# Backward recurrence of a memory transformer: the V pass split 24 and 8 around dS's turning, fill pieces of 4 and 12 products, dout rows spread one step earlier

## The chip, the core and the metric

The kernel runs on one core of a Trainium2 chip. The metric is the device time of one execution in microseconds. A core has five engines that run beside each other: TensorE (PE; its weight loads are listed as PEld), VectorE (DVE), ScalarE (ACT), GpSimd (POOL) and SyncE (SP). Each has a queue of its own and works it off in order; semaphores join them. Matmuls write to PSUM, which has eight banks here: two are held for good by this kernel, six go round among all other sums.

## The reference

The kernel computes the output and all gradients of one pre-norm layer: a recurrent memory attention, then a gated feed-forward block. What the change touches is the gradient of the attention, which runs over the segments from the last to the first.

```python
def _A_ref(x, mem0, Wq, Wk, Wv, Wo, seg_len):        # x 1 x 2048 x 448, 16 heads of 256
    mem = mem0                                        # 8 memory rows
    for s in range(n_seg):                            # 64 segments of 32 rows
        h = concat([mem, x[s * 32:(s + 1) * 32]])     # 40 rows
        q, k, v = h @ Wq, h @ Wk, h @ Wv
        p = softmax(mask(q @ k.T * scale))
        o = (p @ v) @ Wo
        mem = o[:8]                                   # carried to the next segment
        outs.append(o[8:])
h  = x + _A_ref(layernorm(x), ...)
h2 = h + (silu(n @ w_gate) * (n @ w_up)) @ w_down     # n = layernorm(h)
# asked for: h2 and its gradients by x, mem0, Wq, Wk, Wv, Wo, w_gate, w_up, w_down
```

Because the memory rows go from segment to segment, the gradient of segment s needs the memory gradient that segment s+1 hands back: 64 steps in strict order.

## The kernel before, in words

The program has four stages one after the other: the forward recurrence, the feed-forward block with its gradients, the backward recurrence (`backward_chain`), and the weight gradients (`tail_phase`). The order of every engine's instructions is written out by hand: they are issued in the order in which the Python code emits them.

The backward recurrence runs one step per segment, from s = 63 to 0. Four segments make a tile t of 128 rows, and r = s mod 4. A step holds 32 rows that depend on the step before (8 memory rows and the first 24 of the segment); the last 8 rows of each of a tile's four segments (the B rows, 32 per tile) do not depend on the memory gradient of their own step, and their share of the work is done tile by tile, as filling between the pieces of a step. That filling is the dictionary `cur`, with named pieces `ua`, `ub`, `u2`, `u3` for TensorE and `e1`, `e3` for the evacuations; `late` and `late2` hold the transposes of the one and two steps ahead.

- `do_units(t)`: the product of the B rows of dout with Wo, 32 products of 512 columns in two sums; used in the step r = 2 (in segment 61 for the first tile). `u2` opens the second sum `p1`, `u3` closes it.
- `w_units(t, w)`: the B rows' share of the passes with Wv, Wk, Wq (r = 3, 1, 0), 32 products of 448 columns each, added up in the held sum `pob`.
- Segments 63, 62, 60 and 2 have no matmuls of this filling (63 has a piece of the stage before).

One step, in TensorE's order: `ua`; the projection of the gradient rows through Wo (L1364, 2 x 16 products of 512 columns, `proj`); `ub`; its transposes (L1370); the transposes that are late; dP (L1677, 32 products); `outer` for V (L1701, 32 small products into four banks); `u2`; half of the V pass (L1392, `w_pass`, 16 of 32 products of 448 columns; four of them lie side by side in the columns of the array); the turning of dS (L1727, 16 transposes); `outer` for K; the other half of the V pass; `outer` for Q; the K pass and the Q pass (32 products each); `u3`; the turning of the sum (L1399). All three passes add into one bank, `pH`.

The other engines around it: the softmax gradient is four operations of VectorE (L1681 to L1687) between dP and dS's turning. L1355 (VectorE, `V`) and L1358 (ScalarE, `A`) are the evacuations: those of `outer` for V are all ScalarE's, two large casts to dvA, two small ones to the B rows' buffer, and the same again; those for K and Q go to both in turn. `dST` is the evacuated turned dS, which `outer` for Q reads. The sum `pH` is copied in two parts (ScalarE, then VectorE), turned, and added up (L1404, `gsum`), and the memory rows of that go into `dA` for the next step's projection. In the next step VectorE copies the projection `dOev` into `dO_sb` (four copies of 32 x 512, then two), GpSimd does two more (L1652), and both halves of `doT` are filled, the first by VectorE.

GpSimd's queue at a step's start: L1752 copies the new memory rows to `dmem`; L1515 issues the load of P for the step after this one; L1621 copies the B rows of the tile into `doT`, which dP reads; in r = 3, `fill_tile` copies a tile's dout rows from the loaded `xl` to `dB` (L1541) and to the four places of the tile in `dA` (L1542), 24 rows each. `dA` has places for eight segments, so a tile's places are those of the tile two before it.

Of the kernel before, what the change touches and what calls it, by code (L numbers as in the profile page):

```python
# [265 lines left out]
def run_all(k: _K):  # L266
# [128 lines left out]
    with tc.manual_schedule():  # L395
# [83 lines left out]
        WT["o"] = W[3][:, 0:KC * HD].rearrange("p (c n) -> p c n", c=KC)  # L479
        tails = tail_phase(k, tail)  # L480
        back = backward_chain(k, WT, bwd, bwd, rstd1, dmem0T, tails)
        feed = ffn_phase(k, WT, ff, ffn, mv2, rstd2, {"o": Wo2, "v": Wv2, "k": Wk2, "q": Wq2}, back)
        k.feed = feed
# [848 lines left out]
def backward_chain(k: _K, WT, work, stage, rstd1, dmem0T, tails):  # L1332
    nc, tc = k.nc, k.tc
    S, D, M, H, Dh, HD = k.S, k.D, k.M, k.H, k.Dh, k.HD
    SEG, L, NSEG, NT, KC, DP, MC, DC = k.SEG, k.L, k.NSEG, k.NT, k.KC, k.DP, k.MC, k.DC
# [13 lines left out]
    def ps1(dtype=FP32):  # L1349
        if dtype == FP32:  # L1350
            return k.pspool.tile([P, 512], FP32, tag="ps", name="psf")
        return k.pspool.tile([P, 1024], BF16, tag="ps", name="psh")
# [4 lines left out]
    def A(out, in_):  # L1357
        nc.scalar.copy(out=out, in_=in_)  # L1358

    def proj(ps, stat, half, kcs=range(4)):  # L1360
        for kc in kcs:
            for g in range(G):
                c0 = g * GF + half * HB
                nc.tensor.matmul(ps[32 * g:32 * g + 32, :], lhsT=stat(kc), rhs=WoT_sb[:, kc, c0:c0 + HB],  # L1364
                                 start=(kc == 0), stop=(kc == KC - 1))

    def tr_half(ev, half):
        pt = ps1(BF16)
        for j in range(4):
            nc.tensor.transpose(pt[:, j * P:(j + 1) * P], ev[:, half * HB + j * P:half * HB + (j + 1) * P], ident[:, :])  # L1370
        return pt[:, 0:HB].rearrange("p (j g t) -> p j g t", j=4, g=G)

    def fm_view(dst, half, t0, t1):
        return dst[:].rearrange("p (g j) n -> p j g n", g=G)[:, 4 * half:4 * half + 4, :, t0:t1]
# [6 lines left out]
    WoT_sb, WvT_sb, WkT_sb, WqT_sb = WT["o"], WT["v"], WT["k"], WT["q"]  # L1381
    W = [k.Wall[:, i * KC * HD:(i + 1) * KC * HD] for i in range(4)]
    S_ps, pob = k.fix
# [4 lines left out]
    def w_pass(pO, WT, ch, i0, i1, first, last):  # L1388
        for i in range(i0, i1):
            c = ORDER[i]  # L1390
            g = i % 4
            nc.tensor.matmul(pO[32 * g:32 * g + 32, 0:D], lhsT=ch(c), rhs=WT[:, c, :],  # L1392
                             start=(first and i < 4), stop=(last and i >= MC - 4), skip_group_check=True)

    def turn(src, kcs=range(4)):
        y = ps1(FP32)
        for kc in kcs:
            c0 = min(kc * P, D - P)
            nc.tensor.transpose(y[:, kc * P:(kc + 1) * P], src[:, c0:c0 + P], identf[:, :])  # L1399
        return y[:, 0:DP].rearrange("p (c g n) -> p c n g", c=KC, g=G)  # L1400

    def gsum(out, in_):
        with nc.allow_low_precision("four float32 partial sums of one token"):
            nc.vector.tensor_reduce(out=out, in_=in_, axis=AX.X, op=ALU.add)  # L1404
# [11 lines left out]
    def none_units():  # L1416
        return {n: f_none for n in UNITS}

    def do_units(t):
        T = tiles[t]  # L1420
        st = {}

        def stat(kc):
            return T.dB[:, kc, :, :]

        def ua():
            st["p0"] = ps1(FP32)
            proj(st["p0"], stat, 0, range(0, 2))

        def ub():  # L1430
            proj(st["p0"], stat, 0, range(2, 4))

        def e1():
            T.dOB = stage.tile([P, GF], BF16, name="dOBev", tag="dOBev", bufs=2)
            A(T.dOB[:, 0:HB], st["p0"][:, :])

        def u2():
            st["p1"] = ps1(FP32)
            proj(st["p1"], stat, 1, range(0, 2))

        def u3():
            proj(st["p1"], stat, 1, range(2, 4))

        def e3():
            (A if t == NT - 1 else V)(T.dOB[:, HB:GF], st["p1"][:, :])

        def ut():
            T.doTB = stage.tile([P, MC, SEG], BF16, name="doTB", tag="doTB", bufs=2)
            A(fm_view(T.doTB, 0, 0, SEG), tr_half(T.dOB, 0))
            if t == NT - 2:  # L1450
                A(fm_view(T.doTB, 1, 0, SEG), tr_half(T.dOB, 1))

        def ut2():
            if t != NT - 2:
                A(fm_view(T.doTB, 1, 0, SEG), tr_half(T.dOB, 1))
        return dict(ua=ua, ub=ub, e1=e1, u2=u2, u3=u3, e3=e3, ut=ut, et=f_none, ut2=ut2, et2=f_none)

    def w_units(t, which):
        T = tiles[t]
        WT = {"v": WvT_sb, "k": WkT_sb, "q": WqT_sb}[which]  # L1460
        first, last = which == "v", which == "q"

        def ch(c):
            return T.dW[which][:, c, :]

        def ua():
            w_pass(pob, WT, ch, 0, 8, first, last)

        def ub():
            w_pass(pob, WT, ch, 8, 16, first, last)  # L1470

        def u2():
            w_pass(pob, WT, ch, 16, 24, first, last)

        def u3():
            w_pass(pob, WT, ch, 24, 32, first, last)

        def e3():
            A(partB[:, 0:D], pob[:, 0:D])

        if not last:
            return dict(none_units(), ua=ua, ub=ub, u2=u2, u3=u3)

        def half_turn(kcs):
            T.yB = turn(partB, kcs)

        def half_sum(kcs):
            for kc in kcs:
                gsum(T.dxnT[:, kc, :].rearrange("p (r j) -> p r j", r=4)[:, :, XA:SEG],
                     T.yB[:, kc, :, :].rearrange("p (r i) g -> p r i g", r=4))  # L1490
        return dict(ua=ua, ub=ub, e1=f_none, u2=u2, u3=u3, e3=e3, ut=lambda: half_turn((0, 1)), et=lambda: half_sum((0, 1)),
                    ut2=lambda: half_turn((2, 3)), et2=lambda: half_sum((2, 3)))

# [27 lines left out]
    def slot(s):  # L1521
        return s % NWIN

    def new_tile(t):
        o = Tok()
        o.t = t
        tiles[t] = o
        if t == NT - 1:
            o.xl = k.dlast[:].rearrange("p (c r n) -> p c r n", c=KC, r=4)
            return  # L1530
        o.xl = work.tile([P, KC, 4, SEG], BF16, name="dXl", bufs=1)
        if t == NT - 2:
            k.dnext = o.xl[:].rearrange("p c r n -> p (c r n)")
            return
        nc.gpsimd.dma_start(out=o.xl[:].rearrange("p c r n -> p (c r n)"), in_=dr["doutT"][t])

    def fill_tile(t):
        o = tiles[t]
        o.dB = stage.tile([P, KC, 4, M], BF16, name="dBx", tag="dBx", bufs=2)
        eng = nc.vector if t == NT - 1 else nc.gpsimd  # L1540
        eng.tensor_copy(out=o.dB[:], in_=o.xl[:, :, :, XA:SEG])  # L1541
        eng.tensor_copy(out=dA[:, :, slot(4 * t):slot(4 * t) + 4, M:SEG], in_=o.xl[:, :, :, 0:XA])  # L1542

    def open_tile(t):
        T = tiles[t]
        T.dxnT = stage.tile([P, KC, P], FP32, name="dxnT", tag="dxnT", bufs=3)
        T.dA = {w: stage.tile([P, MC, P], BF16, name="d" + w + "A", tag="d" + w + "A", bufs=1) for w in "vkq"}
        T.dmem = stage.tile([P, KC, 4, M], BF16, name="dmem", tag="dmem", bufs=2)
        o0 = MC * D + (t % 2) * MC * SEG
        T.dW = {w: W[i][:, o0:o0 + MC * SEG].rearrange("p (c n) -> p c n", c=MC) for i, w in enumerate("vkq")}  # L1550
# [46 lines left out]
    for s in range(NSEG - 1, -1, -1):  # L1597
        t, r = divmod(s, 4)
# [22 lines left out]
        nc.gpsimd.tensor_copy(out=doT[:, :, SEG:L], in_=T.doTB[:, :, r * M:(r + 1) * M])  # L1621
        if s == NSEG - 1:
            new_tile(t - 1)
        if r == (3 if t + 1 < NT else 2) and t > 0:
            fill_tile(t - 1)
        if r == 1 and t > 1:
            new_tile(t - 2)
# [3 lines left out]
        def stat(kc):  # L1631
            return dA[:, kc, slot(s), :]
# [14 lines left out]
        p1 = ps1()  # L1647
# [23 lines left out]
        for half in range(2):  # L1671
            for h in HEADS[half]:
                gg, hh = divmod(h, HG)
                for dc in range(DC):
                    c = h * DC + dc
# [40 lines left out]
        dvA, dkA, dqA = [T.dA[w][:, :, r * SEG:(r + 1) * SEG] for w in "vkq"]  # L1716
        outer(dO_sb, P_sb, dvA, T.dW["v"], (A, A, A, A), True)
        cur["u2"]()
        pH = ps1()
        w_pass(pH, WvT_sb, lambda c: dvA[:, c, :], 0, 16, True, False)  # L1720
        dST = work.tile([P, HG, L], BF16, name="dST", bufs=1)
        pts = []
        for gg in range(2):
# [5 lines left out]
        V(dST[0:L], pts[0][0:L, 0:HG * L].rearrange("p (h n) -> p h n", n=L))  # L1729
        A(dST[QB:NR], pts[1][QB:NR, 0:HG * L].rearrange("p (h n) -> p h n", n=L))  # L1730
        outer(Q_sb, dS, dkA, T.dW["k"], (V, A, V, A))
        w_pass(pH, WvT_sb, lambda c: dvA[:, c, :], 16, 32, True, False)
        if r == 0:
            nc.gpsimd.dma_start(out=dr["dVA"][t], in_=T.dA["v"][:].rearrange("p c n -> p (c n)"))
        outer(K_sb, dST, dqA, T.dW["q"], (V, A, V, A))
# [12 lines left out]
        if s >= 1:  # L1748
            gsum(dA[:, :, slot(s - 1), 0:M], y[:, :, 0:M, :])
            if r == 0:  # L1750
                open_tile(t - 1)
            nc.gpsimd.tensor_copy(out=tiles[(s - 1) // 4].dmem[:, :, (s - 1) % 4, :], in_=dA[:, :, slot(s - 1), 0:M])  # L1752
        else:
            gsum(dmem0T[:], y[:, :, 0:M, :])
        cur["e3"]()
# [326 lines left out]
```

## Time and profile before

| What | Value |
|---|---|
| Median of 3 runs | 2935.06 us (2926.3 to 2940.95) |
| The profiled execution | 2936.97 us, its span 2935.2 us |
| Mean granted TensorE clock | 0.980 |
| PE, DVE, ACT, POOL busy, of the span | 93%, 53%, 37%, 26% |
| Busy in 1313 to 2268 us (the backward recurrence): PE, DVE, ACT, POOL | 873, 574, 376, 246 us of 955 |
| DMA share in that stretch | 0.60 |

A row of the timeline reads: start, length, engine, line, operation, output<-input, shapes, how many instructions are merged into the row, and in square brackets how long the engine was idle before it and what ended that. Names: `arena` is one large SBUF buffer that holds nearly every tile, `wall` the buffer of the weights, `psf` and `psh` the banks that go round (float32, bfloat16), `s_ps` a held bank. A matmul's end is modelled, its start is measured. In the chain of waits, a row is start, length and the engine with its line, and "issue" is time for which nothing is shown.

### The profile page before, as it was taken

The page shows a single profiled execution, that of the slowest core. Times are in us where ns is not written, and L with a number is a line of the kernel's source. Part 1 is how long each engine was busy: PE and PEld are TensorE (multiplying, and loading weights), DVE is VectorE, ACT ScalarE, POOL GpSimd, SP SyncE. Part 2 cuts the span into 40 slices and gives each one's busy share as a digit, 9 for nine tenths or more (in the row PEclk, how much of TensorE's full clock was granted, in tenths as well). Part 3 has the DMA queues.
Part 4 walks back from the last instruction along what each step waited for, and adds up shares of the span by engine and source line. Part 5 has one row for each costly group of instructions (what it writes and reads, how often), then busy time and mean ns, then how long its engine had stood idle before and what let it go on. Part 6 is the DMA issues. An engine that isn't in the chain of part 4 may idle for free.

```text
span 2935.2 us, 104407 instructions
## 1 busy us (share of the span) xinstructions
PE 2722.7 (93%) x44384; PEld 1514.8 (52%) x44420; DVE 1561.3 (53%) x4196; ACT 1082.5 (37%) x2880; POOL 762.1 (26%) x1420
## 2 busy tenths in 40 slices
PE   3999999999998799987999999999999999999999
PEld 1555555555554455543555555555555454545454
DVE  4666666666665578874666666666665112222221
ACT  2444444444443455552444444434433111111110
POOL 2222222222222223321222222222222222233222
PEclk7999999999999899998999999999999999999999
DMA  9334434343435899997655655565556999999992
GB/s 273 116 123 134 126 123 137 116 130 122 135 116 140 217 218 233 245 226 166 151 156 153 189 152 161 155 175 152 161 151 215 334 228 227 209 225 241 204 224 69
DMA packets 652001, 515.86 MB, mean 176 GB/s; under 512 B 508592, under 2 KB 558112, under 8 KB 642000
## 3 DMA queue, kind: packets, MB, share of 16 engines
q1 hardware_dynamic: 600640, 309.09, 47.5%
q0 software_dynamic: 50896, 200.09, 20.5%
q8 instruction: 350, 5.73, 0.8%
q14 instruction: 115, 0.94, 0.1%
HBM read 145.89 MB, written 230.33 MB: 128 GB/s over the span
## 4 chain that ended last, share of the span: by engine, by line
PE 69%; DVE 15%; DMA 7%; issue 5%; SPq 2%; ACT 2%; POOL 1%; DVEq 0%; ACTq 0%; POOLq 0%
PE psf L1919 13%; PE psf L558 9%; PE psf L1392 9%; DVE arena L1355 5%; PE psf L687 4%; PE psf L1880 4%; PE psf L1105 3%; PE psf L1701 3%; PE psf L566 3%; PE psf L1364 2%; PE psh L572 2%; PE psf L1932 2%; PE psf L910 2%; PE psf L1399 2%; DMA wall<-in_A_Wv_dram 2%
## 5 line engine op out<-in xcount | busy, mean ns | idle before, releaser
L1919 PE MATMUL psf<-wall,arena 128*128 128x512 bf16 (+1 forms) x1788 | 390.6, 373 | 1.9
L521 ACT CAST arena<-psf 128x512 bf16<-128x512 f32 (+2 forms) x560 | 235.8, 453 | 362.4 <-PE psf L558 251.3
L1392 PE MATMUL psf<-wall,arena 128*32 128x448 bf16 x6144 | 336.8, 361 | 17.0 <-DMA wall<-in_A_Wq_dram 11.9
L1358 ACT CAST arena<-psf 128x256 bf16<-128x256 f32 (+1 forms) x597 | 233.0, 417 | 304.2 <-PE psf L1364 214.0
L558 PE MATMUL psf<-wall,arena 112*32 112x512 bf16 x5120 | 308.9, 384 | 31.0 <-DMA wall<-in_A_Wk_dram 14.0
L1919 PEld LDWEIGHTS <-arena 128*128 128x128 bf16 x1824 | 176.2, 98 | 198.3 <-issue 4.7
L1807 DVE CAST arena<-psf 128x448 bf16<-128x448 f32 (+1 forms) x83 | 54.7, 659 | 418.7 <-PE psf L1919 267.1
L518 DVE CAST arena<-psf 128x512 bf16<-128x512 f32 (+2 forms) x432 | 191.8, 469 | 123.7 <-PE psf L558 83.8
L1392 PEld LDWEIGHTS <-arena 128*32 128x32 bf16 x6144 | 154.9, 98 | 135.7 <-issue 30.7
L558 PEld LDWEIGHTS <-arena 112*32 112x32 bf16 x5120 | 126.4, 97 | 161.8 <-issue 28.2
L1355 DVE CAST arena<-psf 128x256 bf16<-128x256 f32 (+1 forms) x339 | 164.8, 486 | 83.0 <-PE psf L1701 41.8
L1805 ACT CAST arena<-psf 128x512 bf16<-128x512 f32 (+1 forms) x75 | 42.2, 563 | 427.9 <-PE psf L1919 267.0
L566 PE MATMUL psf<-wall,arena 112*32 112x512 bf16 x2560 | 169.2, 385 | 9.4 <-DMA wall<-in_A_Wv_dram 9.4
L1364 PE MATMUL psf<-wall,arena 128*32 128x512 bf16 x2560 | 156.6, 381 | 1.2 <-DVE arena L1404 1.2
L521 ACT COPY arena<-psh 40x160 bf16<-40x160 bf16 (+2 forms) x320 | 119.2, 400 | 94.6 <-PE psh L670 52.8
L1752 POOL COPY arena<-arena 128x32 bf16<-128x32 bf16 x63 | 13.2, 210 | 541.5 <-DVE arena L1404 541.5
L1701 PE MATMUL psf<-arena 40*128 40x40 bf16 x6144 | 146.9, 178 | 3.2 <-issue 1.8
L687 PE MATMUL psf<-wall,arena 128*32 128x224 bf16 x5120 | 147.6, 265 | 1.1 <-issue 1.1
L524 POOL COPY arena<-arena 32x512 bf16<-32x512 bf16 x129 | 77.8, 603 | 267.9 <-ACT arena L521 264.2
L1701 PEld LDWEIGHTS <-arena 40*128 40x128 bf16 x6144 | 125.8, 93 | 33.8 <-issue 16.2
L1355 DVE COPY arena<-arena 32x512 bf16<-32x512 bf16 x384 | 133.8, 349 | 8.8
L1355 DVE COPY arena<-psf 128x192 f32<-128x192 f32 x64 | 22.9, 358 | 215.2 <-ACT arena L1358 215.2
(223 smaller groups left out, 4475.5 us busy)
## 6 DMA issues: line engine op xcount, KB each, us to landing
Vtok<-arena SPq DMA_DIRECT2D x128, 192.0 KB
KtokA<-arena SPq DMA_DIRECT2D x64, 256.0 KB
QtokA<-arena SPq DMA_DIRECT2D x64, 256.0 KB
OTA<-arena POOLq DMA_DIRECT2D x16, 1024.0 KB, 5.2
arena<-QtokA SPq DMA_DIRECT2D x128, 128.0 KB
arena<-KtokA SPq DMA_DIRECT2D x128, 128.0 KB
dVA<-arena POOLq DMA_DIRECT2D x16, 1024.0 KB, 5.2
dKA<-arena POOLq DMA_DIRECT2D x16, 1024.0 KB, 7.2
```

What stands on the lines that cost most here:

```text
L518: nc.vector.tensor_copy(out=out, in_=in_)
L521: nc.scalar.copy(out=out, in_=in_)
L558: nc.tensor.matmul(ps[32 * g:32 * g + 32, :], lhsT=stat(kc), rhs=W_sb[0:DB, kc, c0:c0 + HB], start=(kc == 0), stop=(kc == KC - 1))
L566: nc.tensor.matmul(ps[32 * g:32 * g + 32, :].rearrange("t (y d) -> t y d", y=2), lhsT=stat(kc), rhs=wv[:, x, :, half, e, :], start=(kc == ...
L687: nc.tensor.matmul(ps[32 * g:32 * g + 32, 0:2 * DB], lhsT=x, rhs=Wo_sb[:, c, a * 2 * DB:(a + 1) * 2 * DB], start=first, stop=last)
L1355: nc.vector.tensor_copy(out=out, in_=in_)
L1358: nc.scalar.copy(out=out, in_=in_)
L1364: nc.tensor.matmul(ps[32 * g:32 * g + 32, :], lhsT=stat(kc), rhs=WoT_sb[:, kc, c0:c0 + HB], start=(kc == 0), stop=(kc == KC - 1))
L1392: nc.tensor.matmul(pO[32 * g:32 * g + 32, 0:D], lhsT=ch(c), rhs=WT[:, c, :], start=(first and i < 4), stop=(last and i >= MC - 4), skip_gr ...
L1701: nc.tensor.matmul(po[:, n * L:(n + 1) * L], lhsT=lhs[b:b + L, lc:lc + P], rhs=rhs[b:b + L, hh, 0:L], start=True, stop=True)
L1880: nc.tensor.matmul(ps[:, 0:D], lhsT=stat[:, i, c * P:(c + 1) * P], rhs=Y[:, i, 0:D], start=(i == 0), stop=(i == kts - 1))
L1919: nc.tensor.matmul(ps[:, 0:N], lhsT=Hx[:, i, dc * P:(dc + 1) * P], rhs=X[:, i, b * N:(b + 1) * N], start=(i == 0), stop=(i == kts - 1))
```

## The change

Four edits in the backward recurrence.

1. The V pass runs 24 products ahead of dS's turning and 8 behind `outer` for K; it was 16 and 16.
2. `u2` of `do_units` does one quarter of the second sum (4 products) and `u3` three (12); they did 8 and 8.
3. `u2` of `w_units` does 4 products and `u3` 12; they did 8 and 8.
4. The dout rows of a tile are spread (`fill_tile`) at the end of the step ahead, that is in r = 0, behind the copy to `dmem`; it was done in r = 3, behind the copy to `doT`. In segment 62 it stays where it was.

```diff
         def u2():
             st["p1"] = ps1(FP32)
-            proj(st["p1"], stat, 1, range(0, 2))
+            proj(st["p1"], stat, 1, range(0, 1))
         def u3():
-            proj(st["p1"], stat, 1, range(2, 4))
+            proj(st["p1"], stat, 1, range(1, 4))
...
         def u2():
-            w_pass(pob, WT, ch, 16, 24, first, last)
+            w_pass(pob, WT, ch, 16, 20, first, last)
         def u3():
-            w_pass(pob, WT, ch, 24, 32, first, last)
+            w_pass(pob, WT, ch, 20, 32, first, last)
...
-        if r == (3 if t + 1 < NT else 2) and t > 0:
+        if s == NSEG - 2:
             fill_tile(t - 1)
...
-        w_pass(pH, WvT_sb, lambda c: dvA[:, c, :], 0, 16, True, False)
+        w_pass(pH, WvT_sb, lambda c: dvA[:, c, :], 0, 24, True, False)
...
-        w_pass(pH, WvT_sb, lambda c: dvA[:, c, :], 16, 32, True, False)
+        w_pass(pH, WvT_sb, lambda c: dvA[:, c, :], 24, 32, True, False)
...
             nc.gpsimd.tensor_copy(out=tiles[(s - 1) // 4].dmem[:, :, (s - 1) % 4, :], in_=dA[:, :, slot(s - 1), 0:M])
+            if r == 0 and t > 1:
+                fill_tile(t - 2)
```

## The prediction

> **What bounds the kernel now.** I read the page's chain of waits first, then the same chain in order of time for a stretch of the backward recurrence, then the timeline around the lines that the change touches.
>
> ```profile
> PE 69%; DVE 15%; DMA 7%; issue 5%; SPq 2%; ACT 2%; POOL 1%; DVEq 0%; ACTq 0%; POOLq 0%
> ```
>
> The columns are engines and their shares of the chain. TensorE carries 69% of it, and yet 15% runs through VectorE: within one backward step the two alternate. The chain of a plain step (segment 49, r = 1; start, length, engine and line) shows where.
>
> ```profile
> 1541.52 0.50 DVE arena L1687
> 1542.02 0.04 issue
> 1542.06 0.49 PE psh L1727 x16
> 1542.56 0.67 PE psf L1701 x32
> 1543.22 0.87 PE psf L1392 x16
> 1544.09 0.67 PE psf L1701 x32
> 1544.76 3.17 PE psf L1392 x64
> ...
> 1548.00 0.38 ACT arena L1358
> ...
> 1548.43 0.83 PE psf L1399 x4
> ```
>
> From dS (L1687) on, everything up to the step's end is in series: dS is turned (L1727), outer(k), the second half of the V pass (16 products, 0.87), outer(q), the K and Q passes, the copy of the sum, its turning (L1399). So whatever TensorE does between dS's turning and the step's end that could have been done earlier is on the path; what it does while it waits for dS is free. Price of a product of the pass: 48 more of them cost 3.17 - 0.87 = 2.30, so 0.048 each, 0.19 for a group of four, and the 16 in 0.87 hold 0.10 of change-over to the next kind of matmul.
>
> **Part 1: the V pass, 24 before and 8 behind.** Eight products, 8 x 0.048 = 0.38, leave the path behind dS in every step. What must be shown is that they fit ahead of it.
>
> ```profile
> 1540.45 0.56 PE L1392 MATMUL s_ps<-wall 128*32 128x448 bf16 x8
> 1540.84 0.93 PE L1392 MATMUL psf<-wall,arena 128*32 128x448 bf16 x16
> 1542.06 0.49 PE L1727 MATMUL psh<-ident,arena 40*40 40x40 bf16 x16 [0.30 <-DVE arena L1687]
> ...
> 1540.19 0.65 ACT L1358 CAST arena<-psf 128x256 bf16<-128x256 f32 x2 [0.40 <-PE psf L1701]
> 1540.72 0.35 ACT L1358 CAST wall<-psf 128x64 bf16<-128x64 f32 x2
> 1540.93 0.69 ACT L1358 CAST arena<-psf 128x256 bf16<-128x256 f32 x2
> ```
>
> The wait before the turning shows as 0.30, behind the pipeline's tail. By starts, 16 products from 1540.84 are issued by 1541.61, and dS comes for 1542.06: 0.45 free. The fill piece u2 shrinks from 8 to 4 products, so the pass can begin at 1540.45 + 0.19 = 1540.64; 24 products are issued by 1540.64 + 1.15 = 1541.79, with the change-over 1541.89, still 0.17 before dS. Two new waits lie here. The pass starts 0.2 earlier and needs the first cast of dvA: two casts take 0.65 from 1540.19, the first should be done near 1540.56 (estimate, half way and a little); if both were needed, as at worst, it would begin at 1540.84 as now and be through at 1542.09, which costs 0.03. And products 17 to 24 need the third cast (first of the pair at 1540.93, about 1541.35); they come up at 1540.64 + 0.77 = 1541.41. Behind these waits on TensorE stands only the turning, which waits for dS anyway. Cost ahead of dS: nothing, cover 0.17.
>
> Behind dS, outer(q) comes up at 1543.64 instead of 1544.02 and must find banks and its operand.
>
> ```profile
> 1542.65 0.42 ACT L1358 COPY arena<-psh 40x320 bf16<-40x320 bf16 x1 [0.79 <-PE psh L1727]
> ...
> 1543.36 0.22 ACT L1358 CAST wall<-psf 128x64 bf16<-128x64 f32 x1
> ...
> 1543.23 0.21 DVE L1355 CAST wall<-psf 128x64 bf16<-128x64 f32 x1
> ...
> 1543.69 0.21 DVE L1355 CAST wall<-psf 128x64 bf16<-128x64 f32 x1
> ```
>
> dST is complete at 1543.07. If banks go round in the order in which they come free, outer(q)'s four take those freed at 1543.07, 1543.44, 1543.58 and 1543.90, and are wanted at 1543.64, 1543.81, 1543.98 and 1544.15 (0.67 for four): none late, the narrowest by 0.2. The evacuations of outer(q) and the passes behind it move along. So a plain step gains 0.38.
>
> **Part 2: the fill pieces at the end.** u3 has 12 products instead of 8, while the sum is copied.
>
> ```profile
> 1547.72 0.55 PE L1392 MATMUL s_ps<-wall 128*32 128x448 bf16 x8
> ...
> 1591.09 0.60 PE L1364 MATMUL psf<-wall,arena 128*32 128x512 bf16 x8
> 1591.80 0.44 PE L1399 MATMUL psf<-identf,arena 128*128 128x128 f32 x2
> ```
>
> Plain step: 12 x 0.048 from 1547.72 end at 1548.30, with the change-over at 1548.40, and the turning starts at 1548.43 because it waits for ScalarE. Free, by 0.03. In the dout step (r = 2, pieces of 512 columns, 0.055 each) 12 end at 1591.75, with the change-over 1591.85, against 1591.80: 0.05 to 0.08 late.
>
> The dout step is also the one where the front is full.
>
> ```profile
> 1583.59 0.61 PE L1364 MATMUL psf<-wall,arena 128*32 128x512 bf16 x8
> 1584.15 0.94 PE L1392 MATMUL psf<-wall,arena 128*32 128x448 bf16 x16
> ...
> 1583.87 0.35 ACT L1358 CAST wall<-psf 128x64 bf16<-128x64 f32 x2
> ...
> 1585.18 0.39 PEld L1727 LDWEIGHTS <-arena 40*40 40x40 bf16 x16 [0.54 <-DVE arena L1687]
> ```
>
> Its pass starts 0.56 after u2, where eight products of 0.055 fill 0.44. I read this as the wait of pH for a bank: u2's own sum p1, the half-turned dxn and outer(v)'s four hold all six until ScalarE's first small cast (about 1584.10). A shorter u2 then brings nothing: 24 products from 1584.15 end at 1585.30, with the change-over 1585.40, and the turning is 0.22 later than 1585.18. The dout step so gains 0.38 - 0.22 - 0.06 = 0.10.
>
> Sum of both parts: 45 plain steps with fill (r = 3, 1, 0 of tiles 14 to 0) and four without any (63, 62, 60, 2): 49 x 0.38 = 18.6. Dout steps: 14 x 0.10 = 1.4, and segment 61, where no half-turned dxn holds a bank, 0.3. Together 20.3 us.
>
> **Part 3: the spreading of dout one step earlier.**
>
> ```profile
> 1539.13 0.72 PE L1677 MATMUL s_ps<-arena 128*40 128x40 bf16 x32 [0.29 <-POOL arena L1652]
> 1553.32 0.75 PE L1677 MATMUL s_ps<-arena 128*40 128x40 bf16 x32 [0.25 <-POOL arena L1652]
> 1568.11 0.72 PE L1677 MATMUL s_ps<-arena 128*40 128x40 bf16 x32 [0.84 <-POOL arena L1652]
> 1582.25 0.76 PE L1677 MATMUL s_ps<-arena 128*40 128x40 bf16 x32 [0.25 <-POOL arena L1652]
> ...
> 1563.98 0.21 POOL L1752 COPY arena<-arena 128x32 bf16<-128x32 bf16 x1 [3.40 <-DVE arena L1404]
> 1564.51 0.56 POOL L1515 DMA_DIRECT2D arena<-P_all  x1 [0.32 <-issue]
> 1565.07 0.41 POOL L1621 COPY arena<-arena 128x256 bf16<-128x256 bf16 x1
> 1565.40 0.30 POOL L1541 COPY arena<-arena 128x128 bf16<-128x128 bf16 x1
> 1565.64 0.51 POOL L1542 COPY arena<-arena 128x384 bf16<-128x384 bf16 x1
> 1565.73 1.78 DVE L1355 COPY arena<-arena 32x512 bf16<-32x512 bf16 x4
> ...
> 1565.73 0.56 DVE L1355 COPY arena<-arena 32x512 bf16<-32x512 bf16 x1
> ...
> 1566.71 0.64 POOL L1652 COPY arena<-arena 32x512 bf16<-32x512 bf16 x1 [0.57 <-ACT arena L1358]
> ...
> 1580.47 1.18 DVE L1355 COPY arena<-arena 32x512 bf16<-32x512 bf16 x4
> ```
>
> From dP to dP a step takes 14.19 (1539.13 to 1553.32) but 14.79 into the r = 3 step, where dout is spread (L1541, L1542). The reason stands in the VectorE rows: its four copies of dO take 1.78 beside the spreading (1565.73) and 1.18 without it (1580.47), and dP waits for what follows them. (The releaser POOL L1652 is named because its copy ends near by; it writes nothing that dP reads.) The next step, 1568.11 to 1582.25, is 14.14, 0.05 short of 14.19, so 0.05 of the 0.60 comes back. The spreading now goes behind L1752 and ahead of the load of P and the copy to doT in POOL's queue. If they follow without a gap: L1541 and L1542 end at 1564.19 + 0.81 - 0.14 (each copy starts 0.07 before the last one ends) = 1564.86, P's load at 1565.42, doT's copy at 1565.82. It is read by dP at 1568.11; P's load is for a step later: neither is late. By the records doT's copy overlaps VectorE's first copy by 0.09. But the first copy now ends at 1565.73 + 0.56 = 1566.29, 0.30 (1.18 over four) after 1565.99, while L1542's record ends at 1566.15: VectorE is let in some 0.16 before the record's end, and for doT's copy that is 1565.66, in time. The fourth copy then starts near 1566.62, just ahead of POOL's own copies at 1566.71. So I take the whole: 0.60 - 0.05 = 0.55, 14 times, 7.7 us. Bounds: 0.60 if nothing comes back, and 0 if the 0.32 that POOL now idles before L1515 stays in line.
>
> The rows show the two engines shutting each other out rather than sharing. The Trainium skill (SBUF — State Buffer, "Who interferes with whom") says so: a VectorE copy in a two-port mode and a GpSimd instruction hold the port pair in turn, each for its whole length, and who issues first wins. Taken to the letter, doT's copy would hold off VectorE's first copy by 0.09 and part 3 would give 14 x 0.46 = 6.4 instead of 7.7. It also speaks against the move: its box on SWDGE lets a DMA of the POOL queue starve while VectorE copies, and P's load moves 0.9 towards those copies; no run here shows that.
>
> **Sum.** 20.3 + 7.7 = 28.0 us. The profiled execution took 2936.97 (span 2935.2), 0.07% over the median of 2935.06; so 2909 for a profiled one and about **2907** for the median.
>
> **Rivals.**
> A. The spreading gives nothing: its 0.81 plus the 0.32 idle push doT's copy to 1566.1, under VectorE's copies, and the fourth meets POOL L1652 as now. For it: the slack of only 0.1 or so. Against: L1515 starts 0.53 behind L1752's start, and two more copies in between would cover that. Time: 2907 + 7.7 = 2915. The Trainium skill's rule (same page) of who issues first speaks for it.
>
> B. Behind the turning the banks decide, not TensorE: outer(q) waits until all of outer(k) is evacuated. VectorE's last small cast ends at 1543.90 and ScalarE's should be near it, so outer(q) stays at about 1544.0, plain steps win nothing and dout steps lose 15 x 0.28 = 4. For: the bank wait that I read in dout steps. Against: the order of banks counted above. Time: 2935 + 4 - 7.7 = 2931.
>
> C. The other side: the bank wait of the dout step holds in plain steps too, and B holds behind it. Then the pass starts no earlier than ScalarE's first small cast, about 1541.0, 24 products run to 1542.25, the turning is 0.19 late and nothing behind it is won: 49 x 0.19 + 15 x (0.22 + 0.06) = 13.5 lost, 2941 with part 3 and 2949 without. It decides once the pass in plain steps starts later than 1540.81. Against: the pass now starts 0.39 after u2, exactly its eight products.
>
> D. The moved spreading blocks the next projection, which reads the same tile: POOL ends at 1564.86, the projection starts near 1563.9, 1.0 x 14 = 14 lost, 2907 + 7.7 + 14 = 2929. Against: today it is emitted ahead of the projection too, and that one starts long before L1541.
>
> **How the numbers follow.** Forecast as summed 0.60; A 0.22; B 0.06; C 0.07, more than half of it without part 3; D 0.05. A measurement of this kernel tells 0.5%, 14.7 us, from no change: below 2920.4 counts as faster, above 2949.7 as slower. Faster: the forecast, A, and the near ends of B and D, 0.85. Same: the rest of B and D, and C with part 3, 0.10. Slower: C without part 3, and what I do not see, 0.05. The range: runs of before lie 8.8 below and 5.9 above their median, so 2898 at the low end; up to 2922 it holds A and its scatter.
>
> **What would show it.** The wait of L1727 for L1687 falls in plain steps and is gone in dout steps, where L1687 ends before the turning by 0.2 more. Outer(q) follows outer(k) after about 0.49 instead of 0.87. The interval dP to dP is 13.8 in plain steps, also into r = 3, about 14.4 behind dout steps. VectorE's four copies take about 1.2 in every step. Wrong if outer(q) starts with idle time before it on banks, if L1399 waits for TensorE, or if four copies at 1.8 remain.

## Result and the profile after

| What | Before | After | Ratio, 95% interval |
|---|---|---|---|
| Median of 11 runs each, side by side | 2937.65 us | 2916.11 us | 0.994 [0.9918, 0.9962] |
| The changed kernel again (6 runs), beside before (29) | 2925.34 us | 2901.89 us | 0.9909 [0.988, 0.9937] |
| And a third time (6 runs, beside 17) | 2927.35 us | 2902.94 us | 0.991 [0.9889, 0.9932] |

The change is faster by 0.6 to 0.9%, 18 to 27 us by the ratios; the medians differ by 21.5, 23.5 and 24.4 us. The forecast, 28 us, is a ratio of 0.9904: inside the two later intervals, below the first.

The profiled execution of the changed kernel took 2919.64 us, its span 2917.9, which is 17.3 less than before. By the first and the last dP, the backward recurrence runs from 1320.8 to 2233.5 us, 912.6; before it ran from 1313.5 to 2253.75, 940.2. It is 27.6 shorter, but that this comes so near the forecast is in part luck: 5.4 of it lie in the step of segment 63 alone, which took 35.05 here before, 29.65 after, and 28.2 to 30.6 in all other profiles of both kinds. The stages ahead of the recurrence ended 7.3 later in this profile and the tail is 3.0 longer; the change touches neither, and over all profiles of this study the first dP lies between 1302.7 and 1323.5. So one pair of profiles says little by its spans. I read the step's parts first, then the steps, then the sum.

The shares of the chain, the whole kernel after:

```profile
PE 70%; DVE 13%; DMA 7%; issue 5%; SPq 2%; ACT 1%; POOL 1%; another core or an unknown queue 0%; DVEq 0%; ACTq 0%; POOLq 0%
```

VectorE's share fell from 15% to 13%: part of TensorE's work moved beside it. The chain in order of time, the same plain step (segment 49):

```profile
1537.29 0.50 DVE arena L1687
1537.79 0.04 issue
1537.84 0.49 PE psh L1727 x16
1538.33 0.67 PE psf L1701 x32
1538.99 0.49 PE psf L1392 x8
1539.49 0.67 PE psf L1701 x32
1540.15 3.14 PE psf L1392 x64
1543.30 0.57 PE s_ps L1392 x12
1543.86 0.80 PE psf L1399 x4
```

Outer(q) follows outer(k) after 0.49 instead of 0.87, and the turning still starts 0.05 after dS, so 24 products do fit ahead of it. ScalarE's copy has left the chain: u3 with 12 products now ends with it (0.57 from 1543.30), as the 0.03 of cover said. L1399 still starts 0.06 behind the end of that copy (1543.40 to 1543.77), as it did before, so u3 does not hold it back.

The starts of dP, timeline of TensorE:

```profile
1534.90 0.73 PE L1677 MATMUL s_ps<-arena 128*40 128x40 bf16 x32 [0.28 <-POOL arena L1652]
...
1548.71 0.75 PE L1677 MATMUL s_ps<-arena 128*40 128x40 bf16 x32 [0.25 <-POOL arena L1652]
...
1562.53 0.75 PE L1677 MATMUL s_ps<-arena 128*40 128x40 bf16 x32 [0.25 <-POOL arena L1652]
...
1576.34 0.76 PE L1677 MATMUL s_ps<-arena 128*40 128x40 bf16 x32 [0.25 <-POOL arena L1652]
```

The intervals are 13.81, 13.82 and 13.81; the second is the one into r = 3, and TensorE's wait of 0.84 ahead of that dP is now 0.25. Medians over the steps without a stall, by the r of the step in which the interval begins:

| Kernel | r = 3 | r = 2 (dout) | r = 1 | r = 0 (into r = 3) | a tile |
|---|---|---|---|---|---|
| before | 14.14 | 14.48 | 14.19 | 14.80 | 57.61 |
| after | 13.82 | 14.31 | 13.81 | 13.82 | 55.76 |

A tile gains 1.85 us; the prediction's steps make it 3 x 0.38 + 0.10 + 0.55 = 1.79.

The spreading, timeline of GpSimd and VectorE from the end of a step r = 0 into r = 3:

```profile
1559.00 0.21 POOL L1752 COPY arena<-arena 128x32 bf16<-128x32 bf16 x1 [3.40 <-DVE arena L1404]
1559.15 0.29 POOL L1541 COPY arena<-arena 128x128 bf16<-128x128 bf16 x1
1559.38 0.50 POOL L1542 COPY arena<-arena 128x384 bf16<-128x384 bf16 x1
1559.84 0.56 POOL L1515 DMA_DIRECT2D arena<-P_all  x1
...
1560.39 0.41 POOL L1621 COPY arena<-arena 128x256 bf16<-128x256 bf16 x1
1560.75 1.18 DVE L1355 COPY arena<-arena 32x512 bf16<-32x512 bf16 x4
1561.73 1.44 POOL L1652 COPY arena<-arena 32x512 bf16<-32x512 bf16 x2 [0.93 <-ACT arena L1358]
```

GpSimd runs them without a gap (the 0.32 of idle time before L1515 is covered), and VectorE's four copies take 1.18, no longer 1.78. DoT's copy ends at 1560.80 by its record, 0.05 after VectorE's first copy began, and holds nothing off.

The dout step, timeline of TensorE, VectorE and ScalarE:

```profile
1577.69 0.40 PE L1364 MATMUL psf<-wall,arena 128*32 128x512 bf16 x4
...
1577.96 0.35 ACT L1358 CAST wall<-psf 128x64 bf16<-128x64 f32 x2
...
1578.25 1.32 PE L1392 MATMUL psf<-wall,arena 128*32 128x448 bf16 x24 [0.16 <-ACT wall L1358]
...
1578.73 0.49 DVE L1687 SCALAR_TENSOR_TENSOR arena<-arena 104x320 bf16<-104x320 f32 x1
...
1579.50 0.49 PE L1727 MATMUL psh<-ident,arena 40*40 40x40 bf16 x16
...
1585.03 0.82 PE L1364 MATMUL psf<-wall,arena 128*32 128x512 bf16 x12
1585.31 0.37 ACT L1358 COPY arena<-psf 128x256 f32<-128x256 f32 x1 [2.58 <-PE psf L1392]
...
1585.78 0.79 PE L1399 MATMUL psf<-identf,arena 128*128 128x128 f32 x4
```

The profile now names the bank wait that the prediction read: the pass idles 0.16, and what ends it is ScalarE's small cast to `wall`. DS is there at 1579.22 and the turning starts at 1579.50, 0.28 behind it, where a plain step has 0.05: 0.23 late. At the step's end L1399 starts 0.10 after ScalarE's copy (1585.68), where plain steps have 0.06.

One thing the prediction has no term for. Windows from the dP of segment 62 to that of segment 0 (the window, its length, busy time of PE, PEld, DVE, ACT, POOL, granted clock, DMA share, GB/s), before and after:

```profile
1348.60:2253.80 905.20, 841.03 (x19691) 487.16 (x19691) 555.18 (x1560) 363.27 (x1299) 236.83 (x470) 0.99 0.57 158
```

```profile
1350.50:2233.50 883.00, 840.91 (x19691) 487.74 (x19691) 550.76 (x1559) 364.29 (x1300) 238.95 (x472) 0.99 0.60 162
```

TensorE is busy for the same 841 us, so the 22 us are idle time that was taken out. But some idle time has come in. Waits of 1313 to 2268 us, before and after (us, times, longest):

```profile
PEld L1727 <- DVE arena L1687: 43.1, 63, 0.9
...
PE psh L1727 <- DVE arena L1687: 13.6, 48, 0.5
...
PE psf L1392 <- issue: 4.5, 3, 2.2
```

```profile
PEld L1727 <- DVE arena L1687: 31.4, 63, 0.7
...
PE psf L1392 <- issue: 7.0, 6, 3.2
```

The wait for dS fell, as forecast (its second row is gone after). "Issue", time for which nothing is shown, grew: it comes in stalls between like matmuls. One of them, timeline of TensorE, segment 24:

```profile
1892.09 3.02 PE L1392 MATMUL psf<-wall,arena 128*32 128x448 bf16 x58
1897.14 0.55 PE L1392 MATMUL psf<-wall,arena 128*32 128x448 bf16 x6 [2.04 <-issue]
```

Call excess what the intervals from the dP of segment 59 to that of segment 0 hold above the median of their r (that of the steps without a stall, as in the table), where it is over 0.15: 10.7 us in this profile of before, 16.6 in this one of after.

### The profile page after: what moved, and what is told of

Its sections match the earlier page's. It is cut to its first block, busy times and chain, and to the rows that moved or that the text cites. A ratio compares the mean times of both kernels' runs of the same rounds, so it can differ in the third digit from the quotient of the medians.

```text
span 2917.9 us, 104401 instructions
## 1 busy us (share of the span) xinstructions
PE 2727.5 (93%) x44420; PEld 1515.5 (52%) x44420; DVE 1555.8 (53%) x4196; ACT 1082.6 (37%) x2880; POOL 763.4 (26%) x1420
## 4 chain that ended last, share of the span: by engine, by line
PE 70%; DVE 13%; DMA 7%; issue 5%; SPq 2%; ACT 1%; POOL 1%; another core or an unknown queue 0%; DVEq 0%; ACTq 0%; POOLq 0%
PE psf L1921 13%; PE psf L558 9%; PE psf L1392 8%; DVE arena L1355 5%; PE psf L687 4%; PE psf L1105 3%; PE psf L1882 3%; PE psf L1701 3%; PE psf L566 3%; PE psf L1364 3%; PE psh L572 2%; PE psf L1934 2%; PE psf L910 2%; PE s_ps L1392 2%; PE s_ps L1185 2%
## 5 line engine op out<-in xcount | busy, mean ns | idle before, releaser
L1392 PEld LDWEIGHTS <-arena 128*32 128x32 bf16 x6144 | 147.9, 98 | 134.2 <-issue 30.2
```

## The experiments

Theory: each of the four edits does what the prediction's steps say (T). The rivals are A, B, C and D of the prediction.

**One part alone.** E1 has only the split of the V pass (edit 1), e2 only the pieces (edits 2 and 3), e3 only the spreading (edit 4).

```diff
# e1
+        w_pass(pH, WvT_sb, lambda c: dvA[:, c, :], 0, 24, True, False)
...
+        w_pass(pH, WvT_sb, lambda c: dvA[:, c, :], 24, 32, True, False)
# e2
+            proj(st["p1"], stat, 1, range(0, 1))     # u3: range(1, 4)
...
+            w_pass(pob, WT, ch, 16, 20, first, last) # u3: 20, 32
# e3
+            if r == 0 and t > 1:
+                fill_tile(t - 2)
```

> Only edit 1: V pass 24 and 8, pieces 8 and 8, spreading in r = 3 as before. My theory (the pass behind dS's turning is on the path, banks do not decide): with u2 still 8 products the pass begins at the old place, 24 products end 0.03 after dS, so plain steps fall from 14.19 to 13.84 from dP to dP, the step into r = 3 from 14.80 to 14.45, the dout step from 14.48 to about 14.32; sum about 49 x 0.35 + 15 x 0.16 = 19.5 us. Rival (outer(q) waits for the evacuation of outer(k), banks decide): plain steps stay at 14.2 or rise, sum 0 or a loss.

> Only edits 2 and 3: pieces 4 and 12, V pass 16 and 16, spreading as before. My theory: the pass begins 0.19 earlier and waits that much longer for dS, and u3's third group fits into the copy of the sum: plain steps stay at 14.19, the wait of L1727 for L1687 grows by 0.19; the dout step is 0.02 to 0.08 longer; sum 0 to 1 us lost. Rival (TensorE's work at the end is not covered): plain steps 0.19 longer, 9 us lost.

> Only edit 4: dout rows spread at the end of r = 0. My theory: the step into r = 3 falls from 14.80 to 14.19, the one behind it rises by 0.05 to 14.19, VectorE's four copies take 1.2 instead of 1.8; sum 14 x 0.55 = 7.7 us. Rival A (the copy to doT takes the place of the spreading beside VectorE's copies): into r = 3 stays at 14.8, sum 0. Rival D (the projection waits for the spreading): into r = 3 about 15.2.

| Kernel | Ratio, 95% interval | r = 3 | r = 2 | r = 1 | r = 0 |
|---|---|---|---|---|---|
| e1, split | 0.9944 [0.9925, 0.9964] | 13.83 | 14.31 | 13.82 | 14.45 |
| e2, pieces | 1.0019 [0.9997, 1.0042] | 14.14 | 14.48 | 14.19 | 14.80 |
| e3, spreading | 0.9981 [0.9959, 1.0003] | 14.20 | 14.48 | 14.19 | 14.20 |

The split carries the gain of the steps. The pieces change no interval, not even the dout step's, for which 0.02 to 0.08 more had been expected; with the split they are worth about 0.01 in a step (13.83 to 13.82, 13.82 to 13.81). The spreading takes 0.60 out of the interval into r = 3 and gives 0.06 back in the next, as the prediction had it from one place of the old trace. By time alone e3 can't be told from nothing; its intervals can, in the timeline of e3's TensorE:

```profile
1533.96 0.75 PE L1677 MATMUL s_ps<-arena 128*40 128x40 bf16 x32 [0.25 <-POOL arena L1652]
...
1548.16 0.75 PE L1677 MATMUL s_ps<-arena 128*40 128x40 bf16 x32 [0.25 <-POOL arena L1652]
```

These are the dP of segments 48 and 47: 14.20 into r = 3, where before had 14.79 in the same place. A and D fall; C falls with e1, which has no step that is longer than before, and so does B for 24 products, since plain steps do win.

**The bank wait of the dout step.** E5 is the changed kernel with `u2` put behind the 24 products in the dout step, so that `pH` takes its bank ahead of `u2`'s sum.

```diff
+        late_u2 = r == 2 and t > 0 and t + 1 < NT
+        if not late_u2:
-        cur["u2"]()
+            cur["u2"]()
         pH = ps1()
         w_pass(pH, WvT_sb, lambda c: dvA[:, c, :], 0, 24, True, False)
+        if late_u2:
+            cur["u2"]()
```

> The changed kernel, but in the dout steps (r = 2, tiles 14 to 1) pH and its 24 products are emitted ahead of u2, so that pH takes the sixth bank and p1 the next free one. My theory (the pass waits there for a bank): it starts some 0.15 to 0.2 earlier, u2 fits behind it, the turning comes about 0.16 sooner and the dout step falls from 14.31 to 14.15; other steps stay; 2 us in all. Rival (the pass waits for dvA's casts or for the change-over, not for a bank): the pass starts where it did, u2 behind it delays the turning by 0.2 more, 14.5.

Measured: 2899.32 against 2925.73 us, 0.9908 [0.9881, 0.9935], and 14.16 behind dout steps. TensorE's timeline of such a step in e5 (L1731 is the turning):

```profile
1562.46 1.35 PE L1392 MATMUL psf<-wall,arena 128*32 128x448 bf16 x24
1563.64 0.39 PE L1364 MATMUL psf<-wall,arena 128*32 128x512 bf16 x4
1563.96 0.49 PE L1731 MATMUL psh<-ident,arena 40*40 40x40 bf16 x16
```

The pass starts without idle time, and the turning starts 3.00 behind dP (1560.96) instead of 3.16 (1579.50 less 1576.34). So it was the bank. This is the best version of the study by its steps, by 0.15 in each of 14 steps, 2 us; the time does not separate it from the change.

**More products ahead.** E6 runs 28 products ahead of the turning and 4 behind, e7 all 32 ahead. Behind the turning TensorE's own work would shrink by 0.19 and 0.38 more.

```diff
# e6
-        w_pass(pH, WvT_sb, lambda c: dvA[:, c, :], 0, 24, True, False)
+        w_pass(pH, WvT_sb, lambda c: dvA[:, c, :], 0, 28, True, False)
...
-        w_pass(pH, WvT_sb, lambda c: dvA[:, c, :], 24, 32, True, False)
+        w_pass(pH, WvT_sb, lambda c: dvA[:, c, :], 28, 32, True, False)
# e7: 0, 32 and no second w_pass
```

> The changed kernel with 28 products ahead and 4 behind. My theory: in plain steps 28 products end 0.02 to 0.1 after dS and 0.19 leaves the path behind it, banks are still free in time: 13.81 falls to 13.65 to 13.72. In dout steps 0.19 is lost ahead and won behind: 14.31 stays. Together 5 to 8 us faster than the change. Rival B (the banks of outer(k) decide behind the turning): plain steps no shorter, or longer.

> The changed kernel with all 32 products ahead of the turning and none behind. If TensorE alone decided behind the turning: turning 0.2 late, 0.49 won behind it (eight products and a change-over): plain steps 13.54. By my reading of the banks (outer(q)'s last two wait for the third and fourth evacuation of outer(k)): about 13.84, with idle time of TensorE inside outer(q). Dout steps 14.5 to 14.7.

Measured: e6 0.9949 [0.9927, 0.9971], plain steps 13.82 to 13.85, dout 14.39. E7 0.9975 [0.9955, 0.9994], plain steps 14.01 to 14.04, dout 14.58. The gain I expected of e6 did not come, and e7 is worse than I gave it by either reading. The timeline of TensorE and ScalarE in a plain step of e6:

```profile
1539.76 0.37 PE L1392 MATMUL psf<-wall,arena 128*32 128x448 bf16 x4
...
1540.06 0.92 PE L1701 MATMUL psf<-arena 40*128 40x40 bf16 x32
...
1540.34 0.24 ACT L1358 CAST wall<-psf 128x64 bf16<-128x64 f32 x1
...
1540.91 0.75 PE L1392 MATMUL psf<-wall,arena 128*32 128x448 bf16 x12
```

Outer(q) starts 4.34 behind dP (1535.72) in e6 and 4.52 in the changed kernel, 0.18 earlier, but takes until the K pass 0.85 instead of 0.66: all of it is lost again. Its last quarter starts at 1540.63, 0.05 after ScalarE's last small cast of outer(k) ends (1540.58). The same stretch of the changed kernel, TensorE and ScalarE (the last row from a window cut at that point):

```profile
1538.26 0.73 PE L1701 MATMUL psf<-arena 40*128 40x40 bf16 x32
...
1539.42 0.73 PE L1701 MATMUL psf<-arena 40*128 40x40 bf16 x32
1539.50 0.24 ACT L1358 CAST wall<-psf 128x64 bf16<-128x64 f32 x1
...
1540.08 0.75 PE L1392 MATMUL psf<-wall,arena 128*32 128x448 bf16 x12
...
1539.80 0.36 PE L1701 MATMUL psf<-arena 40*128 40x40 bf16 x11
```

There the cast ends at 1539.74 and the quarter starts at about the same 0.05 behind it. So 24 and 8 is just where the banks begin to bind; rival B's mechanism is real, and stands one group of four further on. In e7 nothing lies between the two outer products, and both stand in TensorE's timeline as one row:

```profile
1526.69 0.49 PE L1727 MATMUL psh<-ident,arena 40*40 40x40 bf16 x16
1527.11 1.89 PE L1701 MATMUL psf<-arena 40*128 40x40 bf16 x64
1528.93 2.26 PE L1392 MATMUL psf<-wall,arena 128*32 128x448 bf16 x44
```

1.82 from outer(k)'s start to the K pass, where the changed kernel needs 1.82 with eight products of the V pass between them (1538.26 to 1540.08): the eight products were free there. And the turning is 0.2 late as well (3.14 behind dP at 1523.55, where the changed kernel has 2.94).

**The stalls.** In the eleven profiles of kernels that store tile by tile (all but e8 and e11), every pause of over 0.8 us between the starts of two matmuls of one line lies, in segments 59 to 1, in a step of r = 0, which issues the three stores of a tile's dVA, dKA and dQA, 1 MB each, or in the step r = 3 behind it (43 pauses, 0.8 to 2.7 us). E8 is the changed kernel with these stores moved behind the recurrence, e11 the kernel before with the same. Both store the last tile's buffers in every other tile's place, so they leave out the other tiles' part of the gradients of Wq, Wk and Wv and serve for times alone. Their total times hold the stores at the end and are not compared with the others.

```diff
-        if r == 0:
+        if s == 0:
             nc.gpsimd.dma_start(out=dr["dVA"][t], ...)   # and dKA, dQA
...
+    for tt in range(1, NT):
+        for x in "vkq":
+            nc.gpsimd.dma_start(out=dr["d" + x.upper() + "A"][tt], ...)
```

> The changed kernel, but the stores of dVA, dKA and dQA of tiles 15 to 1 (3 MB each tile, in r = 0) are sent together behind the last step, all from the last tile's buffers; the whole is some 200 us longer for that, only the steps 59 to 0 are read. In six profiles all stalls of TensorE over 0.6 us (issue) lie in steps r = 0 and r = 3. Theory S: the tile's stores bring them: they are gone, excess over the regular steps falls from 12 to 15 us to under 4. Rival: they come from the supply of instructions alone and stay where they are (segments 32, 28, 24).

> The kernel before with the stores of dVA, dKA and dQA of tiles 15 to 1 sent behind the last step (from the last tile's buffers; longer as a whole for that), to be held against the same with the change, whose steps 59 to 0 took 825.1 us with 2.4 of excess. Both theories: regular steps as before (849 us), excess under 4, so 850 to 853 for steps 59 to 0: the whole difference of 25 to 28 us stands where no stalls are.

Measured: 3022.75 us for e8 and 3058.91 for e11 as a whole. From dP of segment 59 to dP of segment 0:

| Kernel | us | excess |
|---|---|---|
| before with its stores at the end (e11) | 849.7 | 1.4 |
| after with its stores at the end (e8) | 825.1 | 2.4 |
| before, mean of two profiles (859.6, 853.5) | 856.6 | 7.8 |
| after, mean of three profiles (838.5, 837.1, 836.6) | 837.4 | 15.5 |

The windows of e8 over that stretch:

```profile
1377.70:2202.80 825.10, 794.02 (x18781) 461.55 (x18782) 525.13 (x1487) 346.35 (x1237) 205.96 (x408) 1.00 0.45 111
```

Without the stores (DMA share 0.45, not 0.60) the change takes 24.6 us out of these 59 steps, and next to no excess is left in either. With them it takes 19.1. So the stalls come with the stores, and 5.5 us of the steps' gain go back into them. Segment 0, whose own stores stay in place in e8 and e11, keeps its pause in all thirteen profiles (1.3 to 3.5 us).

What TensorE lacks in a pause no row of the timeline names, but the trace's DMA packets do. One queue carries instructions (number of packets, MB, share of the 16 engines; the same in before and after):

```profile
q8 instruction: 350, 5.73, 0.8%
```

These 350 packets of 16 KB go with some 89 700 instructions of PE and PEld: 64 bytes each, 256 to a packet. Counted through, TensorE goes on after each of the 43 pauses at the same place of such a block of 256 (instruction 193 or 194), and 1.25 to 1.61 us behind the end of a packet of this queue. So what it waits for is its next instructions. The packets come late: one starts a median of 0.8 to 1.0 us after TensorE has begun the block ahead, but in the eleven profiles 162 start more than 2.5 and up to 5.2 us after that, every one of them in r = 0 or r = 3; in e8 and e11 none starts more than 2.2 after it. A block lasts about 5.7 us. So theory S and its rival are both half of it: the instructions run short, and they do so beside the stores.

**Repeats.** E4 and e10 are the changed kernel again, e9 is the kernel before.

> The changed kernel once more, for a second profile. From dP to dP the steps saved 28 us where nothing unusual happens, but the measured gain is some 20. Theory X: the rest is scatter of TensorE's rare stalls of 1 to 4 us (issue) and of the stages ahead and behind, which differ from execution to execution: the regular steps are again 13.81, 14.31, 13.81, 13.82, the stalls sum to something else than 15 us (before: 11), and the stages outside are within 10 us of both profiles. Theory Y: the denser steps cause more stalls: the sum is again 15 or more.

> The kernel before once more, for a second profile of it. So far the excess of steps 59 to 0 over the regular ones was 10.7, 7.4 and 8.7 us in the three profiles with 16 products ahead, and 15.1, 14.5, 12.0, 10.6, 10.2 and 13.7 in the six with 24 or more. Theory Y (denser steps give part of the gain back as stalls, 3 to 4 us): 7 to 11 here. Theory X (scatter): anywhere from 7 to 15. The ratio is 1.

> The changed kernel a third time, for its ratio: 0.994 [0.9918, 0.9962] and 0.9909 [0.988, 0.9937] so far. Steps alone (28 us) would give 0.9905; with 3 to 4 us of stalls given back (theory Y) 0.9918. The regular steps are 13.81, 14.31, 13.81, 13.82; excess by Y 10 to 15, by X anywhere from 7.

E4 and e10 stand in the first table; their intervals are 13.82, 14.31, 13.81 and 13.82 again. E9 gave 0.9997 [0.9974, 1.0019] against before, which is how well this comparison tells no change. Excess in all profiles with the stores in place: 16 products ahead 10.7, 7.5, 9.7 and 4.8 (before, e2, e3, e9), mean 8.2; 24 or more ahead 16.6, 14.6, 15.1, 12.1, 13.3, 13.7 and 14.6 (after, e1, e4 to e7, e10), mean 14.3. (The expectations give lower figures for some, as 15.1 for after: they count from medians over all steps, and in after, e4, e5, e6 and e10 more than half of the steps of r = 3 hold a stall.) The sets do not meet, so the difference of 6 is not one profile's accident, but its size is uncertain by some us: e9's 4.8 lies below what either theory gave it. That e4 and e10 have 15.1 and 14.6 speaks for theory Y.

## Why the prediction was right, and where it was not

- **The chain, and 0.38 for eight products.** Right: 0.38 in each plain step (14.19 to 13.81; 14.20 in e3 to 13.82 in r = 3 and r = 0), and the split alone brings it. That the turning has cover was right at 24: it starts 2.93 behind dP in both kernels.
- **The dout step.** Right in its mechanism, the bank wait of `pH`: the turning is 0.21 late by the medians (0.23 in the step shown) where 0.22 was forecast, and e5 takes the wait away and gains 0.15. The sum was mis-sized: 0.17 gained (14.48 to 14.31), not 0.10. The term that failed is the 0.06 for the longer u3, which the next item answers; without it, 0.38 less 0.21 is the 0.17.
- **U3 free in plain steps, 0.05 to 0.08 late in dout steps.** Right for plain steps, where its work and ScalarE's copy end together. In the dout step L1399 is 0.05 late as forecast, but that is not on the path: in e2 L1399 starts 9.60 behind dP instead of 9.56 (medians of the dout steps of segments 57 to 6), and the next projection 10.84 behind it as before. The longer u3 costs next to nothing and brings next to nothing: the pieces alone change no interval (e2), and e1 without them is within 0.02 of the change in the steps that the spreading leaves alone.
- **Outer(q)'s banks.** This step failed: "none late, the narrowest by 0.2". Its list of banks ends with VectorE's last small cast (1543.90) and leaves out ScalarE's, and it wants the fourth bank after three quarters of 0.67. The old trace has both otherwise (the second row from a window cut at that point):

```profile
1543.73 0.24 ACT L1358 CAST wall<-psf 128x64 bf16<-128x64 f32 x1
...
1544.39 0.37 PE L1701 MATMUL psf<-arena 40*128 40x40 bf16 x11
```

ScalarE's cast ends at 1543.97, and outer(q)'s last quarter opens 0.37 behind the first product (1544.02), while the quarter ahead of it still runs. With outer(q) at 1543.64 the bank is wanted at 1544.01, and 0.05 behind the cast, as in e6, it is there at 1544.02. So the last quarter has no slack at all at 24 and 8, as the traces of e6 and of the change show. That the forecast of that edit came out is luck: the wanted time and the free time just fall together there. The 0.2 would have allowed e6 another 0.19, and e6 gained nothing.

- **The spreading.** Right to 0.01: 0.60 less 0.06, 14 times 0.54, 7.6 us where 7.7 were forecast. The Trainium skill (SBUF — State Buffer, "Who interferes with whom") has the lock held for the whole instruction, which to the letter of the records would have cost 0.09 a tile. It cost nothing: VectorE's four copies take 1.18 although the first begins 0.05 before GpSimd's record ends. This does not speak against the rule. In the old trace the first copy took 0.56 beside L1542 and 0.28 without it, so it was held, and let in some 0.14 before the end of L1542's record; by both cases the records end a little after VectorE is let in. That who issues first wins, which spoke for rival A, did not come up, since GpSimd was through in time. The load of P was misread: it starts 0.91 ahead of VectorE's first copy where it started 1.22 ahead, so it moved by 0.31 towards it, not by 0.9, and it ends 0.35 ahead of the copies. It takes 0.56 as before; what a load beside those copies would do, no run here shows.
- **The sum.** 1.79 a tile forecast, 1.85 measured, 28 us if every step ran undisturbed. Missing was a term for the stalls around the tile stores: 5 to 6 us given back. With them the expected gain is near 22, which lies between the three measurements of 18 to 27.
- **What stays open.** E8 and e11 show that the stalls go when the stores go, and the packets show that TensorE waits for instructions in them. Why the packets start late beside the stores, no record names. Why the denser recurrence stalls more is not shown by a run of its own; it fits that TensorE uses up a block sooner, so that a packet ends a median of 3.0 to 3.1 us ahead of the next block in the three profiles of the change and 3.3 to 3.4 ahead in the two of before. Of the 0.6% and the 0.9% I can't say which is nearer, beyond their intervals; the stage ahead of the recurrence alone scatters by 21 us between profiles.

## What to carry to other kernels

Work that needs no result of a wait belongs ahead of it; how much of it is found by the chain behind the wait, but also by the banks: the products behind the wait also gave the time in which the next sums' banks were emptied, and past 24 of 32 it paid nothing to move more of them. Check such a bound by one step too many (e6), since a slack that is counted from the old trace can leave out the bank that binds. A small copy of GpSimd beside VectorE's copies between SBUF tiles is worth moving, even by a few tenths, to where VectorE idles or reads PSUM. And judge an edit of a few us by its intervals per step, not by the total, and ask what else runs in the stretch: idle time that is squeezed out of TensorE can come back as waits for instructions beside a large store, and the packets of the instruction queue show them where the timeline shows only "issue".

## What was not expected of the hardware

TensorE stalls for 0.8 to 2.7 us in the middle of a row of like matmuls, only in the steps in which a tile's 3 MB are stored and the steps behind them, and each of these 43 stalls ends at the same place of a block of 256 instructions, 1.25 to 1.61 us behind a packet of the instruction queue; with the stores moved out, 59 steps lose 1.4 to 2.4 us in all. A VectorE copy beside a GpSimd copy can begin 0.05 ahead of the end of GpSimd's record and take no longer than alone (1.18 for four).
